# Decode attention on one core: the last group's output products as three column tiles, and the second last slab folded on GpSimd

## The chip, the core and the metric

The kernel runs on one NeuronCore of a Trainium2 chip. A core has five instruction streams: PE (TensorE, matrix products), DVE (VectorE), ACT (ScalarE), POOL (GpSimd) and SP (SyncE, which here only issues transfers), and 16 DMA engines that bring data from HBM into the core's SBUF. Products land in PSUM, a memory of banks of 512 fp32 columns on 128 partitions. The metric is the device time of one execution in microseconds (us), the median of several runs.

## What is computed

Two independent problems, A and B, of the same shape. Each takes one new token for two batch entries and attends to the last 4096 positions of a key and value cache:

```python
B, Sq, D = 2, 1, 576
Hq, Hkv, Sk, Dh = 32, 16, 16384, 128
W = min(4096, max(256, Sk // 4))            # 4096
q = (x @ wq).reshape(B, Sq, Hq, Dh)         # bf16 throughout
k = k_cache[:, :, Sk - W:, :]               # each kv head serves two q heads
v = v_cache[:, :, Sk - W:, :]
scores = einsum(q, k) * Dh ** -0.5
p = softmax(scores)
o = einsum(p, v)                            # (2, 1, 32 * 128)
result = o @ wo                             # (2, 1, 576)
```

The results of A and B stand side by side in an output of 2 x 1 x 1152 in bf16.

## The kernel before

**Slabs.** A problem's 2 x 16 kv heads are read in eight slabs each for K and V; a slab is four (batch, head) pairs of 4096 positions, 4 MB, laid out as 128 partitions (4 pairs x 32 rows) by 128 positions of 128 numbers. With two problems there are 16 slabs (ND = 16, numbered 0 to 15), and two slabs form a group (NG = 8): group G has slabs 2G and 2G+1 and covers four q heads of each half of the heads, for both batch entries. K and V slabs go through a ring of four SBUF buffers, and SP issues the load of the next slab when the buffer's last reader is done. The order of the loads is the list `stream`; the last V slab (15) comes in two pieces, positions 0 to 95 and 96 to 127 (`PIECES`).

**One slab.** DVE transposes K in four parts (L494), PE makes the scores in PSUM tile `st` (L519, and L171 where the weights stay loaded), DVE takes the maximum (L529), ACT the exponential with its row sums (L564), DVE transposes the probabilities (L572), and PE multiplies them with V into `acc` (L610): 32 matmuls of 512 columns, four at a time on column tiles of 32 partitions in the one bank.

**Folding.** `acc` holds the sum over positions in 4 x 32 rows, of which only the matching blocks count. ACT copies it to `acc_sb` (L622). For every slab but the last two, GpSimd masks the copy with `maskJ` (L629) and adds its four blocks in two steps (L632, L637) into `acc_r`, and PE adds over partitions with `maskS` (`comb`, L650). For slabs 14 and 15, PE does both with four matmuls against columns of `ident_r` (L657). DVE multiplies with the reciprocal sums (`norm`, L674 and L692).

**Output projection.** For every group but the last, the normalised heads are spread by a mask (`spread`, L683), gathered by PE (`redist`, L708) and copied by ACT into `Rsb` (L716), which regroups eight rows of heads so that the group's 1024 rows of wo can be read as long packets (`wob`). PE then multiplies `Rsb` with `wob` (L743 for 512 columns into `ot`, L171 for the other 64 into a small bank `tb`), summed over groups in PSUM and in `o_rest`. The last group (7) is split: slab 14 goes through spread (L696) and `redist` and covers four of the eight rows, slab 15 comes directly from `norm` as `oTn` (four heads). Its products (L747) are two halves of 288 columns: `fin(0)` on PSUM partitions 0 and 1 of the first bank of slab 14's score tile `st`, `fin(1)` on partitions 32 and 33 of its second bank. Before them, the sums of groups 4 to 6 are copied there from `ot` and `tb` by ACT (L767) and DVE (L768, L770), so that the products add to them. Then ACT and DVE copy one half each to `out_sb` (L779, L780), and ACT and SP issue a transfer for each half (L788).

**The last weights.** Behind the two pieces of V 15, SP issues the last group's wo rows: 512 rows for slab 14 (L284), then for the four heads of slab 15 three loads (`HEADS`: heads 0 and 1, head 2, head 3; L268). Head 2's load is split by rows into five transfers (`ROWS`: 8, 4, 2, 2 and 112 rows).

**Order.** Every operation is added to one engine's list with its dependencies, and the lists run in the order of the calls; a wait holds all that stands behind it on its engine. Small PE results alternate between two banks `tb` (`tb_job`), and a job waits until the bank's last result was read. After the loop over slabs, the order is written out by hand:

```python
do_PV(ND - 2, range(NRD), None)
do_comb(D_)                    # slab 13
do_norm(D_)
do_comb(ND - 2)
do_redist(D_ // 2)             # group 6
do_norm(ND - 2)
do_proj(D_)                    # group 6
...
do_PV(D_, ..., pieces[0])      # slab 15
do_redist(D_ // 2)             # group 7, slab 14
do_PV(D_, ..., pieces[1])
do_comb(D_); do_norm(D_)
do_proj(ND - 2); do_proj(D_)
```

Of the kernel before, what the change touches and what calls it, by code (L numbers as in the profile page):

```python
# [59 lines left out]
def build_kernel(nc, probs, out, cfg=None):  # L60
# [30 lines left out]
    NOUT = wo0.shape[1]  # L91
    NH = NOUT // 2
    NB0 = 512
    NB1 = NOUT - NB0
    assert NOUT % 2 == 0 and 0 < NB1 <= NB0
    SCALE = float(Dh) ** -0.5
# [3 lines left out]
    HEADS = [(0, 1), (2,), (3,)]  # L100
    ROWS = [(0, 8), (8, 12), (12, 14), (14, 16), (16, 128)]
    NPC = len(PIECES)

    def by_group(G):
        return G < NG - 1

    es = ExitStack()
    with es:
# [40 lines left out]
        ident_r = sb("ident_r", [128, 32], BF16)  # L149
        out_sb = sb("out_sb", [Bb, NPROB, NOUT], BF16)  # L150
        ps = lambda name, shape: es.enter_context(nc.psum_tensor(name, shape, FP32))
# [12 lines left out]
        wl_sem = [sem("wl%d" % n_) for n_ in range(len(HEADS))]  # L164
        part_sem = [sem("part%d" % n_) for n_ in range(len(ROWS) - 1)]
        out_sem = sem("outdone")
# [18 lines left out]
        def load_x(P, eng):  # L185
# [3 lines left out]

        p_ones_b = S.add("pool", lambda e: e.memset(ones_b[:], 1.0), [], "ones_b")  # L190
        p_ident_b = S.add("pool", lambda e: e.affine_select(ident_b[:], ones_b[:], [[-1, 128]], ALU.is_equal, 0.0,
# [3 lines left out]
        p_ones_f = S.add("dve", lambda e: e.memset(ones_f[:], 1.0), [], "ones_f")  # L195
        p_ident_f = S.add("pool", lambda e: e.affine_select(ident_f[:], ones_f[:], [[-1, 128]], ALU.is_equal, 0.0,
                                                           base=0, channel_multiplier=1), [p_ones_f], "ident_f")
        x_zd = S.add("dve", lambda e: e.memset(x_dup[:].rearrange("b h r t -> b (h r t)"), 0.0), [], "zero_xdup")
# [60 lines left out]
        def issue_last(woP, pc, r0, deps):  # L259
            for n_, hs in enumerate(HEADS):  # L260
                ops = []
                for i, (d0, d1) in enumerate(ROWS if n_ == 1 else [(0, 128)]):
                    sem_h = wl_sem[n_] if d1 == 128 else part_sem[i]

                    def f(e, hs=hs, d0=d0, d1=d1, sem_h=sem_h):
                        t, r = divmod(hs[0], 2)
                        row = t * HH + r0 + 256 + 128 * r
                        return e.dma_start(wob[d0:d1, pc, 4 + hs[0]:4 + hs[0] + len(hs), :],  # L268
                                           woP[row:row + 128 * len(hs), :].rearrange("(h d) n -> d h n", d=128)[d0:d1]).then_inc(sem_h, 16)
                    ops.append(dma_op("sp", sem_h, 1, f, deps, "wl%d_%d" % (n_, i)))  # L270
                wo_last.append(ops)

# [302 lines left out]
        def do_rsel(G):  # L575
            d = [chain[(2 * G, "exp")], chain[(2 * G + 1, "exp")], init["maskS"]]
            if G >= 1:
                d.append(chain[(G - 1, "tot")])
            chain[(G, "rsel")] = S.add("pool", lambda e: e.tensor_tensor(  # L579
                rsel[:, :, :], maskS[:].unsqueeze(1).broadcast_to([128, 2, 8]),  # L580
                rsum[:].unsqueeze(2).broadcast_to([128, 2, 8]), ALU.mult), d, "rsel%d" % G)
# [15 lines left out]
        def do_PV(D_, rounds, wait):  # L597
# [20 lines left out]
            if rounds[-1] == last_r:  # L618
                d = [op]
                if D_ >= 2:  # L620
                    d.append(acc_r_ev[D_ - 2])
                acc_ev[D_] = S.add("act", lambda e: e.activation(acc_sb[:, D_ % 2, :], ACC[:, :], ACTF.Copy), d, "accev%d" % D_)  # L622
                G = D_ // 2
                if not by_group(G) or (D_ % 2 == 0 and G < NG - 2):
                    return
                l0, l1 = (0, 2) if G < NG - 2 else (D_ % 2, D_ % 2 + 1)
                a_ = acc_sb[:, l0:l1, :]
                v = a_.rearrange("k l (j d) -> k l j d", j=4)
                t = S.add("pool", lambda e: e.tensor_tensor(  # L629
                    v, v, maskJ[:].unsqueeze(1).unsqueeze(3).broadcast_to([128, l1 - l0, 4, 128]), ALU.mult),  # L630
                    [acc_ev[2 * G + l] for l in range(l0, l1)] + [init["maskJ"]], "accm%d" % D_)
                t = S.add("pool", lambda e: e.tensor_tensor(a_[:, :, 0:256], a_[:, :, 0:256], a_[:, :, 256:512], ALU.add),  # L632
                          [t], "acca%d" % D_)
                d = [t]
                if G >= 1:
                    d.append(comb[2 * G - 1])
                t = S.add("pool", lambda e: e.tensor_tensor(  # L637
                    acc_r[:, l0:l1, :], a_[:, :, 0:128], a_[:, :, 128:256], ALU.add), d, "accr%d" % D_)
                for l in range(l0, l1):
                    acc_r_ev[2 * G + l] = t  # L640

        def do_comb(D_):
            if by_group(D_ // 2):
                if D_ % 2 == 0:
                    return

                def fg(e, bank):
                    last = None
                    for l_ in range(2):
                        last = e.matmul(bank[:, 8 * l_:8 * l_ + 8], acc_r[:, l_, :], maskS[:, :], start=True, stop=True)  # L650
                    return last
                n, bank, comb[D_] = tb_job(fg, "comb%d" % D_, [acc_r_ev[D_ - 1], acc_r_ev[D_], init["maskS"]])
            else:
                def fl(e, bank):
                    last = None
                    for j4 in range(4):
                        last = e.matmul(bank[:, 0:8], acc_sb[:, D_ % 2, 128 * j4:128 * j4 + 128], ident_r[:, 8 * j4:8 * j4 + 8],  # L657
                                        start=(j4 == 0), stop=(j4 == 3))
                    return last
                n, bank, comb[D_] = tb_job(fl, "comb%d" % D_, [acc_ev[D_], init["ident_r"]])  # L660
            comb_at[D_] = (n, bank)
# [59 lines left out]

        def fin(half):
            return ST[(ND - 2) % 2][32 * half:32 * half + Bb, 512 * half:512 * half + NH]

        def do_proj(D_):
# [8 lines left out]
            else:  # L734
                parts = [([(oTn[:, h, :], 4 + h) for h in hs], [norm[D_]] + wo_last[n_], False, False, n_ == len(HEADS) - 1)
                         for n_, hs in enumerate(HEADS)]
            for lhs, deps, start, rstart, rstop in parts:
                def f(e, rest, lhs=lhs, start=start, rstart=rstart, rstop=rstop):
                    last = None
                    for n_, (l_, s_) in enumerate(lhs):  # L740
# [4 lines left out]
                        else:  # L745
                            for half in range(2):
                                last = e.matmul(fin(half), l_, wob[:, pc, s_, half * NH:(half + 1) * NH],  # L747
                                                start=False, stop=end, skip_group_check=True)
                    return last
                deps = deps + [e_ops[(P - 1, 0)]]  # L750
                if by_group(G):
                    n, bank, proj[D_] = tb_job(f, "proj%d" % D_, deps)
                    rest_at[G] = bank
# [11 lines left out]
                    elif G == NG - 2:  # L765
                        d = [proj[D_], chain[(ND - 2, "exp")], chain[(ND - 2, "max")]]
                        a_ = S.add("act", lambda e: e.activation(fin(0), OT[0:Bb, 0:NH], ACTF.Copy), d, "fin0")  # L767
                        tb_consumer[n] = S.add("dve", lambda e: e.tensor_tensor(  # L768
                            fin(1)[:, NB0 - NH:NH], o_rest[:, :], bank[0:Bb, 0:NB1], ALU.add), d + [rest_add[G - 1]], "fin1")
                        fin_ops.append(S.add("dve", lambda e: e.tensor_copy(fin(1)[:, 0:NB0 - NH], OT[0:Bb, NH:NB0]), [a_], "fin2"))  # L770
                    else:
# [4 lines left out]
        def do_E(P):  # L776
            G = (P + 1) * GPP - 1
            if G == NG - 1:
                e_ops[(P, 0)] = S.add("act", lambda e: e.activation(out_sb[:, P, 0:NH], fin(0), ACTF.Copy), [proj[2 * G + 1]], "Elo%d" % P)  # L779
                e_ops[(P, 1)] = S.add("dve", lambda e: e.tensor_copy(out_sb[:, P, NH:NOUT], fin(1)), [proj[2 * G + 1]], "Ehi%d" % P)  # L780
                return
# [76 lines left out]
        do_comb(D_)  # L858
        do_norm(D_)
        do_comb(ND - 2)  # L860
        do_redist(D_ // 2)
        do_norm(ND - 2)
        do_proj(D_)
        D_ = ND - 1
        issue_until(len(stream) - 1)
        do_PV(D_, range(PIECES[0][0] // JR, PIECES[0][1] // JR), pieces[0])
        do_redist(D_ // 2)
        do_PV(D_, range(PIECES[1][0] // JR, PIECES[1][1] // JR), pieces[1])
# [5 lines left out]
        for P in range(NPROB - 1):  # L874
            do_out(P, 0, NOUT, "sp", [e_ops[(P, 0)], e_ops[(P, 1)]])
        do_out(NPROB - 1, 0, NH, "act", [e_ops[(NPROB - 1, 0)]])
        do_out(NPROB - 1, NH, NOUT, "sp", [e_ops[(NPROB - 1, 1)]])

# [99 lines left out]
```

## Time and profile before

| | |
|---|---|
| time, median of 3 runs | 363.62 us (363.61 to 363.75) |
| the profiled execution's own time | 363.54 us |
| its span, first to last instruction | 362.3 us |
| PE, DVE, ACT, POOL busy | 63%, 56%, 19%, 10% |
| HBM read | 153.10 MB, 423 GB/s over the span |
| mean granted TensorE clock | 0.854 |
| first product of the last group | 358.46 us |
| copies to `out_sb` | 360.52 us |

Times in the profile are counted from the first instruction. A row of a timeline has start, length, engine, line of the kernel, operation and tiles (out<-in), and in square brackets how long the engine was idle before and what ended that. A group of several instructions has xN; its length is then that of the whole group. In a table of stages, each engine has its busy time and in brackets its number of instructions, and the last three columns are the granted clock, the DMA engines' share and their traffic.

### The profile page before, as it was taken

The numbers are of one execution on the slowest core, as the hardware profiler recorded it, in microseconds if no ns is written. First come the engines' busy times: TensorE is split into PE (matmuls) and PEld (weight loads), VectorE is DVE, ScalarE is ACT, GpSimd is POOL, SyncE is SP. The second block draws the span as 40 slices with busy tenths as digits, with TensorE's granted clock in tenths as the row PEclk, the third lists the DMA queues.
The fourth block names the chain that finished last, engine by engine and source line by source line (L and its number), as shares of the span: only waits on it lengthen the run. The fifth ranks groups of instructions, "written<-read, shape, count | busy, mean of one in ns | idle before, by whom it ended". The sixth has DMA issues, their size and how long they took to land.

```text
span 362.3 us, 2770 instructions
## 1 busy us (share of the span) xinstructions
PE 228.3 (63%) x1324; PEld 58.8 (16%) x954; DVE 201.7 (56%) x176; ACT 68.8 (19%) x153; POOL 35.4 (10%) x55
## 2 busy tenths in 40 slices
PE   0398195576866647374874737685672748666774
PEld 0010021112221212111220201111120112211121
DVE  3113598473918476391926557192945739189830
ACT  1046402020300302020200203112120203002131
POOL 1000000003000040004000040001200040100020
PEclk9999589787796969889688968869897897969997
DMA  8999999999999999999999999999999999999995
GB/s 348 416 452 409 459 401 447 438 409 453 422 431 434 420 445 425 438 427 423 431 435 434 431 422 434 434 434 429 411 447 434 434 429 423 431 438 427 436 408 224
DMA packets 7087, 153.27 MB, mean 423 GB/s; under 512 B 794, under 2 KB 1316, under 8 KB 1700
## 3 DMA queue, kind: packets, MB, share of 16 engines
q1 hardware_dynamic: 7068, 153.10, 98.7%
q8 instruction: 9, 0.15, 0.2%
q14 instruction: 2, 0.02, 0.0%
q10 hardware_dynamic: 8, 0.00, 0.0%
HBM read 153.10 MB, written 0.00 MB: 423 GB/s over the span
## 4 chain that ended last, share of the span: by engine, by line
DMA 71%; DVE 14%; PE 14%; SPq 1%; issue 0%; ACT 0%; DVEq 0%
DMA ring<-in_B_k_cache_dram 34%; DMA ring<-in_A_k_cache_dram 26%; DVE xt L494 13%; DMA wob<-in_B_wo_dram 8%; PE st L171 5%; PE st L519 4%; DMA x_sb<-in_B_x_dram 3%; PE st L430 1%; PE ot L171 1%; PE acc L171 1%; PE tb L171 1%; PE tb L430 1%; PE st L747 1%; DVE nM L542 1%; PE tb L532 0%
## 5 line engine op out<-in xcount | busy, mean ns | idle before, releaser
L494 DVE STREAM_TRANSPOSE xt<-ring 128x2048 f32<-128x2048 f32 x64 | 145.4, 2285 | 75.9 <-DMA ring<-in_B_k_cache_dram 39.0
L519 PE MATMUL st<-xt,zq 128*128 128x512 bf16 x256 | 116.8, 456 | 111.4 <-DVE xt L494 85.1
L171 PE MATMUL st<-xt,zq 128*128 128x512 bf16 x256 | 115.4, 451 | 0.0
L519 PEld LDWEIGHTS st<-xt,zq 128*128 128x128 bf16 x256 | 28.1, 110 | 207.5 <-DVE xt L494 99.5
L610 PE MATMUL acc<-ring,pC 128*32 128x512 bf16 x512 | 34.9, 390 | 2.6 <-DMA ring<-in_B_v_cache_dram 2.5
L547 ACT ACTIVATE nMrep<-nM 1x128 f32<-1x128 f32 x16 | 4.9, 308 | 140.1 <-DVE nM L542 140.1
L622 ACT ACTIVATE acc_sb<-acc 128x512 bf16<-128x512 f32 x16 | 9.5, 596 | 80.9 <-PE acc L610 80.9
L572 DVE STREAM_TRANSPOSE pC<-pR 128x1024 bf16<-128x1024 bf16 x16 | 19.5, 1219 | 4.0 <-ACT pR L564 2.1
L529 DVE TENSOR_REDUCE m<-st 128x1 f32<-128x1024 f32 x16 | 19.0, 1190 | 1.4 <-PE st L171 1.4
L629 POOL TENSOR_TENSOR acc_sb<-acc_sb,maskJ 128x1024 bf16<-128x1024 bf16 (+1 forms) x8 | 13.4, 1681 | 60.6 <-ACT acc_sb L622 60.6
L481 POOL TENSOR_TENSOR zq<-qk,maskA 128x128 bf16<-128x128 bf16 x16 | 6.4, 401 | 125.9 <-PE st L171 104.5
L564 ACT ACTIVATE pR<-st,bias_sb 128x1024 bf16<-128x1024 f32 x16 | 17.8, 1114 | 0.5
L454 DVE STREAM_TRANSPOSE qtr<-qrow 128x512 f32<-128x512 f32 x8 | 5.7, 711 | 21.0 <-ACT qrow L444 13.7
L395 ACT ACTIVATE st<-maskB 128x1024 f32<-128x1024 bf16 x16 | 16.5, 1032 | 1.6 <-POOL rsel L579 0.4
L743 PE MATMUL ot<-wob,Rsb 128*2 128x512 bf16 x56 | 15.9, 402 | 0.3 <-DVE om L696 0.3
L610 PEld LDWEIGHTS acc<-ring,pC 128*32 128x32 bf16 x512 | 13.1, 97 | 16.4 <-DMA ring<-in_B_v_cache_dram 3.2
L579 POOL TENSOR_TENSOR rsel<-maskS,rsum 128x16 f32<-128x16 bf16 x8 | 1.7, 218 | 124.0 <-ACT pR L564 124.0
L171 PE MATMUL tb<-wob,Rsb 128*2 128x64 bf16 x56 | 11.1, 199 | 0.0
L362 PE MATMUL tb<-ident_b,x_sb 4*128 4x4 bf16 x4 | 0.3, 174 | 14.2 <-DVE x_dup L369 14.2
L632 POOL TENSOR_TENSOR acc_sb<-acc_sb 128x512 bf16<-128x512 bf16 (+1 forms) x8 | 8.2, 1031 | 0.6
L762 DVE TENSOR_TENSOR o_rest<-o_rest,tb 2x64 f32<-2x64 f32 x3 | 0.6, 209 | 13.8 <-PE tb L171 13.8
L542 DVE TENSOR_REDUCE nM<-tb 1x8 f32<-1x128 f32 x16 | 4.4, 273 | 6.4 <-PE tb L532 6.4
(83 smaller groups left out, 109.6 us busy)
## 6 DMA issues: line engine op xcount, KB each, us to landing
ring<-in_A_k_cache_dram SPq DMA_DIRECT2D x8, 4096.0 KB, 30.7
ring<-in_A_v_cache_dram SPq DMA_DIRECT2D x8, 4096.0 KB, 32.6
ring<-in_B_k_cache_dram SPq DMA_DIRECT2D x8, 4096.0 KB, 30.7
ring<-in_B_v_cache_dram SPq DMA_DIRECT2D x7, 4096.0 KB, 32.4
wob<-in_A_wo_dram SPq DMA_DIRECT2D x4, 1152.0 KB, 33.8
ring<-in_A_wq_dram SPq DMA_DIRECT2D x1, 4096.0 KB, 12.8
ring<-in_B_wq_dram SPq DMA_DIRECT2D x1, 4096.0 KB, 22.5
wob<-in_B_wo_dram SPq DMA_DIRECT2D x3, 1152.0 KB, 33.5
```

What stands on the lines that cost most here:

```text
L171: return e.add_instruction(mybir.InstMatmult(name=nc.get_next_instruction_name(), engine=i.engine, ins=[e.lower_ap(rhs), i.ins[1]], outs=[ ...
L395: chain[(s, "fill")] = S.add("act", lambda e: e.activation(ST[s % 2][:, :].rearrange("k (h j) -> k h j", h=2), maskB[:].unsqueeze(1).broad ...
L494: Xop[(s, u)] = S.add("dve", lambda e: e.transpose(xt[:, i % NKT, :].rearrange("k (j w) -> k j w", w=64), ring[:, n % NR, :].bitcast(FP32) ...
L519: first = last = e.matmul(bank, zq[:, p4, s % NZQ, w0:w0 + 128], mv, start=False, stop=stop, skip_group_check=True)
L529: chain[(s, "max")] = S.add("dve", lambda e: e.tensor_reduce(m1[:, 0:1], ST[s % 2][:, :], AX.X, ALU.max), d, "max%d" % s)
L564: chain[(s, "exp")] = S.add("act", lambda e: e.activation(pR[:, :], ST[s % 2][:, :], ACTF.Exp, bias=bias_sb[:, 0:1], scale=SCALE, accum_ou ...
L572: chain[(s, "pC")] = S.add("dve", lambda e: e.transpose(pC[:, s % NPT, :, :].rearrange("k j c -> k (j c)"), pR[:, :]), d, "pC%d" % s)
L610: last = e.matmul(ACC[32 * cb:32 * cb + 32, 0:512], pC[:, D_ % NPT, j0_:j0_ + 4, :].rearrange("k j c -> k (j c)"), ring[:, n % NR, j0_ * 1 ...
L622: acc_ev[D_] = S.add("act", lambda e: e.activation(acc_sb[:, D_ % 2, :], ACC[:, :], ACTF.Copy), d, "accev%d" % D_)
L629: t = S.add("pool", lambda e: e.tensor_tensor(v, v, maskJ[:].unsqueeze(1).unsqueeze(3).broadcast_to([128, l1 - l0, 4, 128]), ALU.mult), [a ...
L632: t = S.add("pool", lambda e: e.tensor_tensor(a_[:, :, 0:256], a_[:, :, 0:256], a_[:, :, 256:512], ALU.add), [t], "acca%d" % D_)
L743: first = e.matmul(OT[0:Bb, 0:NB0], l_, wob[:, pc, s_, 0:NB0], start=start and begin, stop=end, skip_group_check=True)
```

## The change

- The last group's products run as three tiles of 192 columns (`NT`, `NTC`) on PSUM partitions 0, 32 and 64 of one bank, in place of two of 288 in two banks. The sums of the earlier groups are copied there by three ACT copies and one DVE addition, which now waits for the last of the copies; the DVE copy that followed goes.
- One DVE copy takes all three tiles, partitions 0 to 65, to a new buffer `out_t`. Two transfers, one on SP and one on ACT, each bring one batch entry out, three pieces of 192 numbers.
- Slab 14 is folded on GpSimd by the same three instructions as slabs 12 and 13, and its `comb` becomes one matmul. In the order by hand, the group 6 steps come first, then `comb`, `norm` and `redist` of slab 14, all of it ahead of slab 15's PV products. Some small PE jobs stay on the bank that the job before them used.
- Head 2's weights come as one transfer; `ROWS` and its semaphores go.
- At the start, `ones_b` is filled by DVE and `ident_f` is a DVE copy of `ident_b`; both were GpSimd's. `rsel` of groups 0 and 7 goes from GpSimd to DVE.

```diff
+    NT = 3
+    NTC = NOUT // NT
...
-    ROWS = [(0, 8), (8, 12), (12, 14), (14, 16), (16, 128)]
...
-        p_ones_b = S.add("pool", lambda e: e.memset(ones_b[:], 1.0), [], "ones_b")
+        p_ones_b = S.add("dve", lambda e: e.memset(ones_b[:], 1.0), [], "ones_b")
...
+        p_ident_f = S.add("dve", lambda e: e.tensor_copy(ident_f[:], ident_b[:]), [p_ident_b], "ident_f")
...
-            chain[(G, "rsel")] = S.add("pool", lambda e: e.tensor_tensor(
+            chain[(G, "rsel")] = S.add("pool" if 0 < G < NG - 1 else "dve", lambda e: e.tensor_tensor(
...
+            elif D_ < ND - 1:
+                n, bank, comb[D_] = tb_job(lambda e, bank: e.matmul(bank[:, 0:8], acc_r[:, 0, :], maskS[:, :], start=True, stop=True),
+                                           "comb%d" % D_, [acc_r_ev[D_], init["maskS"]])
...
-        def fin(half):
-            return ST[(ND - 2) % 2][32 * half:32 * half + Bb, 512 * half:512 * half + NH]
+        def fin(t):
+            return ST[(ND - 2) % 2][32 * t:32 * t + Bb, 0:NTC]
...
-                            for half in range(2):
-                                last = e.matmul(fin(half), l_, wob[:, pc, s_, half * NH:(half + 1) * NH],
+                            for t in range(NT):
+                                last = e.matmul(fin(t), l_, wob[:, pc, s_, t * NTC:(t + 1) * NTC],
                                                 start=False, stop=end, skip_group_check=True)
...
-                        a_ = S.add("act", lambda e: e.activation(fin(0), OT[0:Bb, 0:NH], ACTF.Copy), d, "fin0")
+                        for t in range(NT):
+                            c0, c1 = t * NTC, min((t + 1) * NTC, NB0)
+                            a_ = S.add("act", lambda e, t=t, c0=c0, c1=c1: e.activation(fin(t)[:, 0:c1 - c0], OT[0:Bb, c0:c1], ACTF.Copy), d, "fin%d" % t)
                         tb_consumer[n] = S.add("dve", lambda e: e.tensor_tensor(
-                            fin(1)[:, NB0 - NH:NH], o_rest[:, :], bank[0:Bb, 0:NB1], ALU.add), d + [rest_add[G - 1]], "fin1")
-                        fin_ops.append(S.add("dve", lambda e: e.tensor_copy(fin(1)[:, 0:NB0 - NH], OT[0:Bb, NH:NB0]), [a_], "fin2"))
+                            fin(NT - 1)[:, NTC - NB1:NTC], o_rest[:, :], bank[0:Bb, 0:NB1], ALU.add), [a_, rest_add[G - 1]], "finr")
+                        fin_ops.append(tb_consumer[n])
...
-                e_ops[(P, 0)] = S.add("act", lambda e: e.activation(out_sb[:, P, 0:NH], fin(0), ACTF.Copy), [proj[2 * G + 1]], "Elo%d" % P)
-                e_ops[(P, 1)] = S.add("dve", lambda e: e.tensor_copy(out_sb[:, P, NH:NOUT], fin(1)), [proj[2 * G + 1]], "Ehi%d" % P)
+                e_ops[(P, 0)] = S.add("dve", lambda e: e.tensor_copy(
+                    out_t[0:32 * (NT - 1) + Bb, :], ST[(ND - 2) % 2][0:32 * (NT - 1) + Bb, 0:NTC]), [proj[2 * G + 1]], "Eout%d" % P)
...
+        do_fold(ND - 2)
+        do_redist(D_ // 2)
+        do_proj(D_)
         do_comb(ND - 2)
-        do_redist(D_ // 2)
         do_norm(ND - 2)
-        do_proj(D_)
+        do_redist(ND // 2 - 1)
...
-        do_redist(D_ // 2)
...
-        do_out(NPROB - 1, 0, NH, "act", [e_ops[(NPROB - 1, 0)]])
-        do_out(NPROB - 1, NH, NOUT, "sp", [e_ops[(NPROB - 1, 1)]])
+        for b in range(Bb):
+            P = NPROB - 1
+            dma_op("act" if b else "sp", out_sem, 1, lambda e, b=b: e.dma_start(
+                out[b, 0, P * NOUT:(P + 1) * NOUT].rearrange("(t c) -> t c", t=NT), out_t[b:32 * (NT - 1) + b + 1:32, :]).then_inc(out_sem, 16),
+                [e_ops[(P, 0)]], "out%d_b%d" % (P, b))
```

`do_fold` holds the three GpSimd instructions that stood at the end of `do_PV` (L629 to L640), unchanged but for being callable for slab 14.

## Prediction

> **What bounds the kernel now.** I read the page first, for the engine and DMA shares, then the chain of waits over the last 40 us, then the timeline of the last 15 us, then a table of busy times by stage.
>
> The page's DMA rows say that the kernel is one long read: every slice between the first and the last is at 9 tenths, and the traffic is 153 MB at 423 GB/s.
>
> ```profile
> span 362.3 us, 2770 instructions
> ...
> PEclk9999589787796969889688968869897897969997
> DMA  8999999999999999999999999999999999999995
> ```
>
> No engine is near full (PE 63%, DVE 56%, GpSimd 10%), so an edit before the last slab lands is worth nothing unless it delays the issue of a transfer; K slabs land 30.7 us after their issue, which is how much delay the queue swallows. Only what follows the reads can be saved. The chain of waits shows that tail (start, length, what):
>
> ```profile
> 330.00 28.42 DMA wob<-in_B_wo_dram
> 358.42 0.04 issue
> 358.46 2.04 PE st L747 x16
> 360.49 0.02 issue
> 360.52 0.45 DVE out_sb L780
> ```
>
> After 358.42 there are 2.04 us of wo products, 0.45 us of copy, and then 1.3 us for the output's flight to the span's end at 362.27. The timeline shows the products in two batches, and the last transfer's issue:
>
> ```profile
> 332.97 0.43 SPq L268 DMA_DIRECT2D wob<-in_B_wo_dram  x1
> 358.46 1.06 PE L747 MATMUL st<-wob,Rsb 128*2 128x288 bf16 x8
> 359.34 1.13 PE L747 MATMUL st<-wob,oTn 128*2 128x288 bf16 x8
> 360.52 0.40 ACT L779 ACTIVATE out_sb<-st 2x288 bf16<-2x288 f32 x1 [2.46 <-PE st L747]
> 360.52 0.45 DVE L780 CAST out_sb<-st 2x288 bf16<-2x288 f32 x1 [1.95 <-PE st L747]
> ```
>
> In the second batch pairs start every 0.24 us (359.55, 359.79, 360.03): the two halves run side by side, and 288 columns in 240 ns is 1.2 columns per ns. The clock is the reason; the stage table shows it granted at 1.00 up to 358.56 and 0.50 after (the column behind the x counts):
>
> ```profile
> 355.15:358.56 3.41, 1.74 (x28) 0.60 (x22) 0.16 (x1) 0.78 (x2) 0.00 (x0) 1.00 0.91 332
> 358.56:361.98 3.42, 1.92 (x16) 0.63 (x12) 0.46 (x2) 0.40 (x1) 0.00 (x0) 0.50 0.13 44
> ```
>
> One more clock matters, the landing of the last weights (head 3): issue 332.97 plus 26.8 from the page of DMA issues is 359.75 us. The last pair starts at 360.03, so it is PE-bound by 0.28 us only. That caps what faster products can give.
>
> **The change, part by part.**
>
> *Three tiles instead of two.* Removed: 8 pairs of 288 columns; added: 8 trios of 192, with 24 weight loads for 16. At half clock a trio should take 192/1.2 = 160 ns if three tiles stream side by side as two do. That four can, in one bank, is seen in the PV products: 32 matmuls of 512 columns on 32-column tiles take 1.91 us at full clock, 215 ns for each four, with four loads inside. So the first four heads run from 358.46 to about 359.07. Heads 0 and 1 wait for their weights: issue 330.64 plus 28.6 is 359.2; they start at 359.25 and 359.41, head 2 at 359.57. Head 3 is ready at 359.73, but its weights are not: from here the transfer, not PE, sets the start.
>
> *The removed row split.* Head 2's weights come as one transfer of 128 rows, where 16 rows went ahead in four small ones. Most late queues then carry 8 of its rows where they carried 7. A row's packet of 1152 B takes 51 ns in the trace, one every 47 ns, so head 3 lands at 359.80 instead of 359.75. Both ends: 0 (if the split's own overhead balances it) and 0.09 (one packet where packets were slowest, at 86 ns). I take 0.05. Four SP issues of about 0.3 us go; they lie 26 us ahead of their landing, worth nothing.
>
> *The last trio and its end.* It starts 0.04 us after the landing (the first pair did: 358.42 to 358.46), at 359.84. A 288-column matmul lasts 0.444 us at half clock; 96 columns less at 0.833 ns is 0.364. With 0.01 for the third tile it ends at 360.21, against 360.47 before: 0.26 us gained. If trios kept the pairs' 240 ns, head 3 would start at 360.03 as now, and only the shorter last matmul, 0.07, would be left.
>
> *One copy.* Before, ACT and DVE each copied 288 columns, DVE being later (0.45). Now DVE alone reads 66 partitions by 192 columns. DVE's PSUM copies here: 2x64 0.212, 2x224 0.391, 2x288 0.449; between the first two a column costs 1.12 ns, so 192 cost 0.355. Partitions do not count: the 128x1024 reduction takes 1.19, or 1.04 ns a column plus what every instruction carries. Gain 0.09, with ends of 0.08 and 0.12. The Trainium skill (TensorEngine Tiling, "PSUM Bottleneck") advises to share the emptying of PSUM between ScalarE and VectorE after tiling, and the change does the reverse. The same section also advises vectorizing over tiles; if instead the 576 columns cost in sequence, the copy would be an estimated 0.78 us, and the sum would be a loss of 0.07.
>
> *The output.* Two issues stay, one on ACT and one on SP, now both behind the DVE copy; each moves three pieces of 384 B, not two of 576 B. Of the two before, SP's came last, issued at 360.99 and ending the span 1.27 us later. ACT's, issued 0.05 earlier, no longer has a head start but is no later than SP's. A third piece of about 28 ns per issue bounds the cost above at 0.06, a parallel start below at -0.05; I take -0.02.
>
> *The fold of slab 14 on GpSimd.* Four small matmuls go from PE; three GpSimd instructions come: 1.04, 0.67 and 0.43 us by the rows of the neighbouring slab. They can start when ACT has emptied the slab at 349.56 and end at 351.75. PE needs them only after the products of slab pair 6, which end at 352.66, so 0.9 us covers them.
>
> *The moved redistribution.* It now stands ahead of slab 15's PV products on PE, so it can hold them. It waits for a chain: three ACT copies after 352.70 instead of one (0.30 + 0.30 + 0.26, from 2x288 0.362 and 128x16 0.174), then DVE's addition, which now waits for them (0.22), and behind it in DVE's queue the norm (0.16) and the spread (0.42), then PE (0.2): 354.75 with handovers. The first PV piece, which started at 354.30 on its landing, then runs 354.75 to 356.25. The second lands at 356.75, so the cover is 0.5 us; if it were gone, the end would move only after another 0.3 us, since the first four heads finish 0.2 us ahead of the next weights and PE has 0.1 to spare at head 3.
>
> *The rest.* ones_b to DVE and ident_f as a DVE copy lie before 5 us, and DVE then idles 9.7 us for x. rsel on DVE for pairs 0 and 7 adds some 0.2 us ahead of a transpose; its PV products wait for a landing 6 us later. Nothing.
>
> **Sum.** Products 0.26, copy 0.09, rest 0: 0.35; with 0.02 for the output (about half of what its parallel start may save) 0.37. The span goes from 362.27 to 361.90. The profiled execution took 363.54, 1.27 beyond its span, and the median of the runs is 0.08 above it: 363.62 - 0.37 = 363.25 us.
>
> **Rivals.**
>
> *The clock stays full.* The window that preceded the drop had 1.74 us of PE work, the one before it 1.77 and no drop; the change shifts about 0.45 us of PV into the later one. Then the last trio lasts 0.193 + 128 x 0.417 = 0.246 us (from 64 columns 193 ns and 512 columns 380 ns at full clock) in place of 0.364: 363.13. Against it: other windows with 1.4 to 1.9 us went either way. Chance 0.25.
>
> *Small output pieces cost a second trip.* In the trace the pieces leave at 361.7 to 361.8 and the span ends at 362.27, so a write and its answer take some 0.45 us. Were a piece of 384 B read, merged and written, I would add that once: 363.70. No row here shows such a write. The Trainium skill (DMA: Bandwidth & Descriptors, "Specifications") gives 512 B as the least size at line rate, with read-modify-write below, so it speaks against the change. By that rule the gain would be lost. Chance 0.08.
>
> *The tiles take turns in one bank.* Before, the two halves wrote two banks; now three tiles write one. If they took turns, a head would need 3 x 160 = 480 ns at half clock; from 358.46 the eight would end at 362.5, 2.0 us later than 360.47; less 0.09 for the copy that is 365.55, clearly slower. It decides from 0.25 us a head: 358.46 + 7 x 0.25 + 0.37 is 360.58, the old end plus the copy's gain. Against it: the four PV tiles in one bank. Chance 0.04.
>
> *The weights land later.* If the reads end 0.3 us later than worked out (uneven queues without the split, slower packets), the PE part of the gain is gone and the copy stays: about 363.55. Chance 0.08.
>
> **How the numbers follow.** The forecast as summed has 0.45. The last 0.10 is for the stream of reads itself, which I can't work out: it ends up to 1 us earlier or later because another build meets the queues otherwise. A difference of 0.2% is 0.73 us, about what a measurement of this kernel can tell from no change; the forecast is half of that. Faster by over 0.2% needs the full clock, a shorter copy and an earlier landing together, or a better stream: 0.24. Slower by over 0.2% needs the turns, the chain ahead of PV running over, or a worse stream: 0.14. Within: 0.62. The range goes from the full clock with 0.3 us of better landing, 362.80, to the second trip with small losses, 363.80.
>
> **What would show it.** Right: L747's successor has 24 matmuls with trios 160 ns apart in the first batch; the last trio begins 0.04 us after the last wob landing near 359.8; one DVE copy of 66x192 near 0.35 us; both output issues start together; the redistribution near 354.6 and PV's second piece still ended by its landing. Wrong: the last trio directly behind the one before (PE still the bound), a granted clock of 1.00 to the end, PV held beyond 356.8, or a flight of over 1.3 us after the copy.

## The result, and the profile after

The change made the kernel slower: 366.56 us (median of 6 runs, 364.93 to 367.5) against 363.69 for the kernel before, measured with it, a ratio of 1.0075 [1.0053, 1.0098]. Forecast was 363.25, within 362.8 to 363.8.

The profiled execution took 366.49 us with a span of 364.5, so 1.99 lie outside the span, where it was 1.27. The page, with the rows shown of before (the last DMA slice falls from 5 tenths to 3: the reads are over earlier in a longer span):

```profile
span 364.5 us, 2773 instructions
...
PE 225.8 (62%) x1328; PEld 58.4 (16%) x959; DVE 202.1 (55%) x179; ACT 69.0 (19%) x154; POOL 36.5 (10%) x54
...
PEclk9999699897886989889696969889688968869986
DMA  8999999999999999999999999999999999999993
```

The tail of the chain of waits (start, length, what) no longer begins with a landing. From 350.27 until the output is issued it is one row of compute steps:

```profile
350.27 1.17 DVE om L685
...
354.98 0.28 ACT st L771
...
356.18 0.44 DVE om L698
...
356.67 0.22 PE tb L710 x2
356.88 3.37 PE acc L605 x24
...
360.28 0.61 ACT acc_sb L617
...
360.93 0.26 PE tb L659 x4
361.18 0.78 PE st L749 x24
...
361.99 0.35 DVE out_t L783
```

Line 685 is the spread product of group 6 (L683 before), 698 the spread of slab 14, 710 the redistribution, 605 slab 15's PV products, 749 the wo products. The last weights land at 359.69 by the page of DMA issues (359.74 before); the products, which they should have set, start at 361.11, since PV is done at 360.22 only. The timeline of the same execution has the two ends of the story:

```profile
350.11 1.04 POOL L628 TENSOR_TENSOR acc_sb<-acc_sb,maskJ 128x512 bf16<-128x512 bf16 x1 [0.41 <-ACT acc_sb L617]
350.27 1.16 DVE L685 TENSOR_TENSOR om<-oTg,maskD 128x256 bf16<-128x256 bf16 x1
...
361.44 0.50 PE L749 MATMUL st<-wob,oTn 128*2 128x192 bf16 x12
361.99 0.35 DVE L783 CAST out_t<-st 66x192 bf16<-66x192 f32 x1 [0.60 <-PE st L749]
362.37 0.82 SPq L883 DMA_DIRECT2D out_dram<-out_t  x1
362.38 0.81 ACTq L883 DMA_DIRECT2D out_dram<-out_t  x1
```

DVE's product took 0.43 us before (349.58). Here GpSimd's mask product of slab 14, which the change added, had started 0.16 us earlier, and DVE's takes 1.16: it ends 0.28 after GpSimd's. At the other end, each output issue takes 0.82 us instead of 0.25. In the table of stages (PE, PE loads, DVE, ACT, GpSimd; then granted clock, DMA share, GB/s) the clock falls in between:

```profile
349.65:353.06 3.41, 1.50 (x13) 0.65 (x9) 1.40 (x3) 0.56 (x2) 2.24 (x4) 1.00 1.00 428
353.06:356.48 3.42, 2.00 (x11) 0.48 (x4) 0.59 (x3) 0.79 (x3) 0.00 (x0) 0.50 0.92 376
356.48:359.89 3.41, 3.23 (x34) 1.25 (x34) 0.13 (x1) 0.18 (x1) 0.00 (x0) 0.50 0.61 222
359.89:363.30 3.41, 1.34 (x36) 0.69 (x28) 0.52 (x2) 0.60 (x1) 0.00 (x0) 1.00 0.00 0
```

The difference of the two executions, 2.95 us, adds up as follows: the products end 1.46 later (361.94 for 360.48), the copy is 0.10 shorter, from the copy's end to the span's end it is 0.84 longer (2.16 for 1.31), 0.72 lies outside the span, and 0.03 is handover.

### The profile page after: what moved, and what is told of

It is laid out like the page before. It is cut to its first block, busy times and chain, and to the rows that moved or that the text cites. A ratio compares the mean times of both kernels' runs of the same rounds, so it can differ in the third digit from the quotient of the medians.

```text
span 364.5 us, 2773 instructions
## 1 busy us (share of the span) xinstructions
PE 225.8 (62%) x1328; PEld 58.4 (16%) x959; DVE 202.1 (55%) x179; ACT 69.0 (19%) x154; POOL 36.5 (10%) x54
## 4 chain that ended last, share of the span: by engine, by line
DMA 63%; DVE 17%; PE 16%; ACT 2%; issue 1%; POOL 1%; SPq 0%; DVEq 0%; ACTq 0%
DMA ring<-in_B_k_cache_dram 34%; DMA ring<-in_A_k_cache_dram 26%; DVE xt L489 14%; PE st L172 6%; PE st L514 4%; DMA x_sb<-in_B_x_dram 3%; PE st L425 1%; PE acc L605 1%; PE ot L745 1%; PE tb L172 1%; ACT pR L559 1%; DVE m L524 1%; PE ot L172 1%; PE tb L425 1%; PE acc L172 1%
## 5 line engine op out<-in xcount | busy, mean ns | idle before, releaser
L628 POOL TENSOR_TENSOR acc_sb<-acc_sb,maskJ 128x1024 bf16<-128x1024 bf16 (+1 forms) x9 | 14.5, 1608 | 94.0 <-ACT acc_sb L617 94.0
L745 PE MATMUL ot<-wob,Rsb 128*2 128x512 bf16 x56 | 16.8, 419 | 0.3 <-ACT Rsb L718 0.3
L631 POOL TENSOR_TENSOR acc_sb<-acc_sb 128x512 bf16<-128x512 bf16 (+1 forms) x9 | 9.0, 995 | 0.7
```

Of the source, the lines that this page charges most:

```text
L628: t = S.add("pool", lambda e: e.tensor_tensor(v, v, maskJ[:].unsqueeze(1).unsqueeze(3).broadcast_to([128, l1 - l0, 4, 128]), ALU.mult), [a ...
L745: first = e.matmul(OT[0:Bb, 0:NB0], l_, wob[:, pc, s_, 0:NB0], start=start and begin, stop=end, skip_group_check=True)
```

## The experiments

Three costs had to be separated: the chain ahead of PV, the output's issue, and the time outside the span. Each row compares with the kernel before on the same chip (its medians: 363.56 to 363.87 us; span 362.2 to 362.4; outside 1.3). "Outside" is a run's time less its span.

| label | what | median us [range] | ratio [95%] | span | outside |
|---|---|---|---|---|---|
| after | the change | 366.56 [364.93, 367.5] | 1.0075 [1.0053, 1.0098] | 364.6 | 1.97 |
| e1_redist_back | after, redistribution back between the PV pieces | 364.63 [364.36, 365.30] | 1.0016 [1.0003, 1.0030] | 362.6 | 2.00 |
| e9_fold_waits | after, GpSimd's product waits for DVE's | 364.63 [363.96, 364.89] | 1.0018 [1.0001, 1.0035] | 362.6 | 1.99 |
| e2_fold_pe | after, slab 14 folded on PE | 365.53 [364.11, 365.90] | 1.0034 [1.0017, 1.0051] | 363.9 | 1.61 |
| e3_out_by_tile | after, output tile by tile | 364.04 [363.57, 366.08] | 1.0013 [0.9993, 1.0033] | 362.0 | 1.98 |
| e4_two_tiles | after, two tiles | 366.23 [364.22, 366.76] | 1.0044 [1.0022, 1.0066] | 364.5 | 1.95 |
| e7_tiles_batch_out | before + tiles, output by batch entry | 364.05 [363.88, 365.54] | 1.0008 [0.9994, 1.0023] | 362.8 | 1.28 |
| e8_tiles_tile_out | before + tiles, output tile by tile | 363.57 [363.34, 366.00] | 0.9998 [0.9976, 1.0020] | 362.25 | 1.29 |
| e11_piece_pairs | before + tiles, output in unlike pairs | 364.02 [363.95, 364.30] | 1.0002 [0.9990, 1.0015] | 362.75 | 1.31 |
| e6_start_alone | before + moves at the start | 363.86 [363.56, 365.63] | 1.0009 [0.9991, 1.0027] | 362.25 | 1.62 |
| e10_four_memsets | before + four idle DVE fills | 364.18 [363.57, 365.61] | 1.0012 [0.9997, 1.0027] | 362.25 | 2.01 |
| e5_fold_alone | before + fold and order | 363.61 [363.24, 365.38] | 1.0005 [0.9987, 1.0024] | 362.3 | 1.25 |
| e12_start_and_fold | e6 + e5 | 364.24 [363.57, 365.98] | 1.0019 [1.0000, 1.0038] | 362.3 | 1.93 |
| e13_three_mended | after, all three costs removed | 363.40 [363.17, 363.58] | 0.9989 [0.9975, 1.0003] | 362.1 | 1.29 |

### The chain ahead of PV: e1, e2, e9

e1 leaves the whole chain as it is, but PV no longer stands behind it:

```diff
-        do_redist(ND // 2 - 1)          # after do_norm(ND - 2)
...
         do_PV(D_, range(PIECES[0][0] // JR, PIECES[0][1] // JR), pieces[0])
+        do_redist(D_ // 2)
```

> The changed kernel with one step put back: slab 14's redistribution stands between the two PV pieces again, as before the change; fold, tiles and output stay changed. Theory 1 (the redistribution, queued ahead of PV behind a chain that ends at 356.7, holds the PV products until they run at half clock, 356.8 to 360.2): the PV products start at their landing near 354.4 and end near 357.5, the wo products end about 1.3 to 1.6 us earlier, time near 365.1. Rival 2 (the loss is the output alone): time stays at 366.5. Rival 3 (the clock, not the queue): PV starts early but the time falls by less than 0.5.

The median span fell from 364.6 to 362.6 (ten runs). In the timeline PV starts on its landing again, at full clock, the products end at 360.05, and the output's issue is as long as ever:

```profile
354.31 1.48 PE L605 MATMUL acc<-ring,pC 128*32 128x512 bf16 x24 [1.64 <-DMA ring<-in_B_v_cache_dram]
...
359.04 1.01 PE L749 MATMUL st<-wob,oTn 128*2 128x192 bf16 x12
360.48 0.82 SPq L883 DMA_DIRECT2D out_dram<-out_t  x1
```

The profile alone doesn't show that the new place did it. In this execution slab 13 ended early and DVE's product was first, as it was before the change:

```profile
349.48 0.43 DVE L685 TENSOR_TENSOR om<-oTg,maskD 128x256 bf16<-128x256 bf16 x1
349.64 1.16 POOL L628 TENSOR_TENSOR acc_sb<-acc_sb,maskJ 128x512 bf16<-128x512 bf16 x1 [0.74 <-ACT acc_sb L617]
```

Slab 14's spread ended at 354.23, so PV would hardly have been held in the order of the change either. e2 and e9 keep the redistribution ahead of PV. e2 takes slab 14 off GpSimd:

```diff
-        do_fold(ND - 2)
...
-            elif D_ < ND - 1:           # do_comb: one matmul on acc_r
```

> The changed kernel with slab 14 folded on PE by four matmuls again (no GpSimd work after slab 13's), the order by hand as changed. Theory 2 (the fold on GpSimd slows DVE's mask product of group 6, L685, from 0.43 to 1.16 us, because both use the same way into SBUF): L685 back at 0.43, the redistribution 0.7 us earlier or more, time down by 0.7 to 1.5, near 365.3. Rival (the fold is covered): L685 still over 1 us, or the time unchanged at 366.5.

Slab 13 ended late here, as in the change: the product of line 685 (682 here) started at 350.18. It took 0.42 us again, the redistribution came at 354.98 and PV ran from 355.12 at full clock. The time hardly followed, though. In the profiled execution the lateness came from elsewhere: one of 16 transfer queues landed its part of the weights 1.4 us after the others, and the products waited for it.

```profile
361.10 0.64 PE L746 MATMUL st<-wob,oTn 128*2 128x192 bf16 x6 [1.23 <-DMA wob<-in_B_wo_dram]
```

The profiles of e8 and e10 show the same wait (1.46 and 1.41 us). Of 108 executions of the kernel before, 24 have spans of 363.3 or more, longer by about as much, but none of them was profiled. In e2 eight of ten spans were long, and one of them was profiled. So e2 clears the chain in its profile and leaves its own time open. e9 asks the same without moving work: GpSimd's product of slab 14 waits for DVE's.

```diff
-                [acc_ev[2 * G + l] for l in range(l0, l1)] + [init["maskJ"]], "accm%d" % D_)
+                [acc_ev[2 * G + l] for l in range(l0, l1)] + [init["maskJ"]]
+                + ([spread[G - 1]] if D_ == ND - 2 else []), "accm%d" % D_)
```

> The changed kernel with one wait more: GpSimd's mask product of slab 14 waits until DVE's mask product of group 6 (L685) is done, so that DVE always goes first. The redistribution stays ahead of PV. Theory 2 (the chain is late because GpSimd, where it starts first, makes DVE take 1.16 us, and the idle PE then loses its clock): L685 at 0.43 in every clock phase, the redistribution near 354.5 to 355.3, PV at full clock, time as with the redistribution put back, 364.6. Rival (the queue position alone): the chain still ends after 356 and the time stays near 366.5.

```profile
349.45 0.42 DVE L685 TENSOR_TENSOR om<-oTg,maskD 128x256 bf16<-128x256 bf16 x1
350.03 1.04 POOL L628 TENSOR_TENSOR acc_sb<-acc_sb,maskJ 128x512 bf16<-128x512 bf16 x1 [1.15 <-DVE om L685]
...
354.39 1.48 PE L605 MATMUL acc<-ring,pC 128*32 128x512 bf16 x24
```

All eight spans lie at 362.9 or below, their median 2.0 us under the change, with the redistribution still ahead of PV (354.25) and the fold still on GpSimd. The profile is no test of the wait, though: slab 13 ended early, and slab 14's copy was done at 349.58 only, so DVE would have been first without it. The test with a late slab 13 is e13, below. Against e9, the change's redistribution is 2.42 us later (356.67): 0.82 because slab 13 ended later in that execution, 0.73 in the product itself, and 0.85 because the clock fell at 353.06 while the products of group 6 were running (from their start to ACT's copy 3.01 us, not 2.16). Then PV, at half clock, took 3.41 us.

### The output: e3, e4, e7, e8, e11

e3 sends the same three tiles as three transfers, each of two pieces from neighbouring partitions:

```diff
-        for b in range(Bb):
-            P = NPROB - 1
-            dma_op("act" if b else "sp", ..., out_t[b:32 * (NT - 1) + b + 1:32, :] ...)
+        for t in range(NT):
+            dma_op("act" if t == 1 else "sp", ..., out_t[32 * t:32 * t + Bb, :] ...)
```

> The changed kernel with the last output as three transfers of 2 pieces of 384 B (one for each tile; SP, ACT, SP) in place of two of 3 pieces. Theory 3a (three pieces make the issue long: 0.82 us, not 0.25): issues near 0.25 each, span after the copy near 1.5 us in place of 2.1, time down by 0.5. Theory 3b (pieces of 384 B are what costs): issue and flight stay long, time unchanged or 0.2 up. Theory 3c (code loading near the end): issues long in whichever instruction comes first, and the time beyond the span stays at 2.0.

Each issue took 0.25 to 0.26 us, not 0.82. The median span, 362.0, fell further than this explains: in the profiled execution DVE's product was first (349.44, 0.43 us), so the chain was not late either. Up to its output e3 is the change itself, and eight of its ten spans lie at 362.7 or below. So which product comes first is not fixed by the order of the work, and the short spans of e1 and e9 are weaker evidence than they look. e4 goes the other way, with two pieces of 576 B per transfer, 32 partitions apart:

```diff
-    NT = 3
+    NT = 2
```

> The changed kernel with two tiles of 288 columns in one bank in place of three of 192: two ACT copies ahead, 16 matmuls, one DVE copy of 34x288, two transfers of 2 pieces of 576 B. Theory 3a and 3b: issues 0.25, flight after the copy 1.3; the copy 0.45; time down by about 0.7. If the time beyond the span is tied to the output it falls from 2.0 to 1.25 as well, and the time by 1.4. Theory 3c: no change in issue or beyond the span. Theory 1 adds 0.3 us at most, as the ACT copies are two.

```profile
362.41 0.45 DVE L783 CAST out_t<-st 34x288 bf16<-34x288 f32 x1 [0.91 <-PE st L749]
362.88 0.62 SPq L883 DMA_DIRECT2D out_dram<-out_t  x1
```

0.62 us for two pieces of the size that took 0.25 before: neither their number alone nor their size is the reason. The chain was lost here as in the change (DVE's product 1.15, PV 3.60 us from 356.73), which repeats it without the three tiles. e7 and e8 put the tiles on the kernel before, with the two forms of output (edit abridged):

```diff
+    NT = 3; NTC = NOUT // NT            # fin(t), three matmuls, one copy to out_t
+        for b in range(Bb): ...         # e7: as the change
+        for t in range(NT): ...         # e8: as e3
```

> The kernel before with the three tiles, the one copy and the output by batch entry as changed (pieces from partitions 32 apart); order, fold, weights and start as before. Theory 3 (an issue costs 0.2 us for each piece that comes from a partition 32 away, as 2 pieces cost 0.60 and 3 cost 0.82): issues of 0.82, 2.1 us from the copy's end to the span's end, the wo products 0.3 us shorter, span near 362.6. Time 363.9 if 1.3 lies beyond the span, 364.6 if the output makes it 2.0. Rival (the output cost came from the late chain): issues of 0.25, span near 361.9, time 363.2.

> As the run with tiles and output by batch entry, but the output goes in three transfers, one for each tile, two pieces from neighbouring partitions each. Theory 3: issues of 0.26, 1.55 us from the copy's end to the span's end, span near 361.9, time 363.2, 0.4 below before and the best of all. Rival 3b (pieces under 512 B cost): a longer flight, 2.1 us, no better than the other output.

e7's timeline has the products' end at 360.3, the copy to 360.66 and the issue of 0.82 again, and its span ends 2.16 us after the copy:

```profile
360.69 0.82 SPq L883 DMA_DIRECT2D out_dram<-out_t  x1
```

By the medians, e7's span is 0.55 longer than e8's. e8's profile is of an execution with a late queue (products held 1.46 us by a landing), but its output can be read: issues of 0.25, 0.26 and 0.25, the span's end 1.5 us after the copy and 1.2 after the last issue. e11 tells number from neighbourhood: on e7, SP first sends partitions 0 and 33 together and ACT 64 and 65, then each one single partition (edit in words).

```diff
+   sp:  out_t[0:34:33, :]        act: out_t[64:66, :]
+   sp:  out_t[1:2, :]            act: out_t[32:33, :]
```

> The kernel before with three tiles and one copy, and the output in four transfers: SP first takes the pieces of partitions 0 and 33 (which lie apart in the output too), ACT partitions 64 and 65, then SP partition 1 alone and ACT partition 32 alone. Theory 3s (the long issue comes from source partitions that are not neighbours): SP's first issue 0.60, ACT's first 0.26, the single ones below 0.26. Theory 3d (it comes from pieces that join up in the output): SP's first 0.26 too.

```profile
360.69 0.72 SPq L885 DMA_DIRECT2D out_dram<-out_t  x1
360.69 0.25 ACTq L885 DMA_DIRECT2D out_dram<-out_t  x1
```

Two pieces from partitions 0 and 33 cost 0.72, two from 64 and 65 cost 0.25, single ones 0.27 (ACT) and 0.41 (SP). A transfer from SBUF rows that aren't neighbours is what takes long to issue here; why the two single ones differ stays open.

### Outside the span: e6, e10

e6 takes the moves alone: `ones_b`, `ident_f` and two `rsel` on DVE (edit abridged).

```diff
-        p_ones_b = S.add("pool", ...memset(ones_b[:], 1.0)...)
+        p_ones_b = S.add("dve", ...memset(ones_b[:], 1.0)...)
-        p_ident_f = S.add("pool", ...affine_select(ident_f...)...)
+        p_ident_f = S.add("dve", ...tensor_copy(ident_f[:], ident_b[:])...)
+            rsel: "pool" if 0 < G < NG - 1 else "dve"
```

> The kernel before with only the moves off GpSimd: ones_b and ident_f at the start and rsel of groups 0 and 7 on DVE. Theory 1 and 3 give nothing: span 362.3, 1.3 beyond it, time as before within 0.2. Rival 4 (the moves lengthen what lies outside the span, by another split of instructions over the engines): span 362.3, 2.0 beyond it, time 0.7 up.

The span stayed at 362.25 and the time outside it rose from 1.3 to 1.62: half of the change's excess. Its page has 180 DVE instructions for 176. e10 adds only four DVE fills of a buffer that nobody reads:

```diff
+        for i in range(4):
+            S.add("dve", lambda e, i=i: e.memset(pad[:, 2*i:2*i+2], 0.0), [], "pad%d" % i)
```

> The kernel before with four DVE memsets of 128x2 more, at the start, where DVE is idle; nothing uses them. Theory 4a (time beyond the span grows with DVE's number of instructions, 180 to 184, as in the run with the start alone): 1.65 beyond the span, time 0.35 up. Theory 4b (it is what the moved instructions are, or GpSimd's fewer ones): 1.3 beyond the span, time as before.

```profile
PE 225.6 (62%) x1323; PEld 58.0 (16%) x954; DVE 201.6 (55%) x180; ACT 68.7 (19%) x153; POOL 35.3 (10%) x55
```

2.01 us outside, the whole of the excess. Over all kernels the time outside is 1.3 where DVE has 176 instructions or fewer (e5, e7, e8, e11, e13), 1.6 where it has 179 or 180 and GpSimd 51 (e2, e6), and 2.0 where DVE has as many and GpSimd 54 or 55 (the change, e1, e3, e4, e9, e10, e12). That four more DVE instructions are enough is shown by e10, whose own two forecasts (1.65 or 1.3) both missed. Whether it is their number or their place is not shown, since e6, e10 and the change all add some at the start. Neither is what they cause, nor whether GpSimd's count matters or only goes along with it.

### The fold without the rest: e5, e12

In words:

```diff
 e5:  before + do_fold, do_comb and the order by hand of the change
 e12: e5 + the moves of e6
```

> The kernel before with one part of the change alone: slab 14 folded on GpSimd and the order by hand as changed (redistribution ahead of PV); tiles, output, weights and start as before. Theory 1 with 2 (GpSimd's mask product and DVE's mask product of group 6 race; where GpSimd starts first DVE needs 1.16 us, the chain ends late, and PV follows at half clock): two kinds of runs, spans near 362.3 and near 364, and a profile that shows which came first on the side of its span. Rival (the chain is late through the three ACT copies): all runs near 362.3, time as before. Beyond the span: 1.3 if it hangs on output or start, 1.7 to 2.0 if on GpSimd's three instructions.

> The kernel before with the start moves and slab 14's fold with its order, no tiles, no new output, weights in five. Beyond the span: 2.0 if start and fold together make it (theory 4c, as 1.65 with the start alone, 1.3 with the fold alone), 1.65 if the rest of the change (output, single transfer of weights) brings the last 0.35. Spans near 362.2, and near 363.7 where PV meets the half clock or a transfer queue is late.

e5 is where the theory of the race had to give way in part. GpSimd's product was first, DVE's took 1.20, and PV started at 356.49, as late as in the change. Nothing was lost:

```profile
349.69 1.04 POOL L633 TENSOR_TENSOR acc_sb<-acc_sb,maskJ 128x512 bf16<-128x512 bf16 x1 [0.45 <-ACT acc_sb L622]
349.81 1.20 DVE L690 TENSOR_TENSOR om<-oTg,maskD 128x256 bf16<-128x256 bf16 x1
...
356.49 1.91 PE L610 MATMUL acc<-ring,pC 128*32 128x512 bf16 x32
```

PV took 1.91 us at full clock and was done at 358.40, ahead of the last weights; the span is 362.2. e12 shows the same (product 1.16, PV 356.26 to 358.17, span median 362.3). The clock differs from the change: in e5 it was half from 352.21 to 355.62 only, during the products of group 6, and in e12 it stayed at 1.00 from 326.7 until after the last product. So in these two profiles a late PV at full clock cost nothing, and in the change and e4 it met the half clock and cost the time. All profiles fit a loss that needs both, but no run moved the clock alone. Three of e5's ten spans and two of e12's lie near 364; none of them was profiled, so what lengthened them is open.

### All three mended: e13

The change with e9's wait, e3's output, and the moves of e6 undone (edit abridged):

```diff
+                + ([spread[G - 1]] if D_ == ND - 2 else []), "accm%d" % D_)
+        for t in range(NT): ...         # output as e3
-        p_ones_b, p_ident_f, rsel on DVE
+        p_ones_b, p_ident_f, rsel on GpSimd
```

> The changed kernel with the three costs found taken out at once: GpSimd's mask product of slab 14 waits for DVE's of group 6, the output goes tile by tile in three transfers, and ones_b, ident_f and rsel are GpSimd's again; the fold on GpSimd, the order, the tiles, the one copy and the single transfer of weights stay. If the three are all of it: span 361.9, 1.3 beyond it, most runs near 363.2 to 363.3, level with before or 0.1 to 0.3 below it. If something else is left in the change: over 363.9.

```profile
350.50 0.42 DVE L686 TENSOR_TENSOR om<-oTg,maskD 128x256 bf16<-128x256 bf16 x1
351.07 1.04 POOL L629 TENSOR_TENSOR acc_sb<-acc_sb,maskJ 128x512 bf16<-128x512 bf16 x1 [1.15 <-DVE om L686]
...
355.43 2.08 PE L606 MATMUL acc<-ring,pC 128*32 128x512 bf16 x32
...
359.83 0.25 PE L750 MATMUL st<-wob,oTn 128*2 128x192 bf16 x3 [0.16 <-DMA wob<-in_B_wo_dram]
360.12 0.35 DVE L784 CAST out_t<-st 66x192 bf16<-66x192 f32 x1 [1.45 <-PE st L750]
360.50 0.56 SPq L884 DMA_DIRECT2D out_dram<-out_t  x2
```

363.40 us, 3.2 below the change, and all twelve spans at 362.3 or below: with the three costs away nothing of the loss is left. Slab 13 ended late here too (DVE's product at 350.50), and slab 14's copy was done at 350.31. In the change GpSimd started 0.08 after that copy, so without the wait it would have been first again by about 0.1. With the wait there was no collision, the redistribution came at 355.30 and PV ran at full clock. This profile and e2's are the ones that show the collision at work: late slab 13, no collision, no loss in the chain. Against the kernel before the ratio is 0.9989 [0.9975, 1.0003]: 0.16 us less, which can't be told from no change. The last trio does start on the landing of the weights and lasts 0.25, as one rival had it, and the copy ends 0.50 earlier than in the profile of before (360.47), but 0.22 of that is given back between it and the span's end (1.53 for 1.31), where SP now has two issues in a row (0.56).

## Why the prediction was wrong

- **Failed: "0.9 us covers them" for the fold, and the chain ahead of PV.** The three GpSimd instructions did have their cover; what I didn't ask was which DVE instruction would run beside the first of them. The trace of before had the answer: I took 349.56 as GpSimd's start, and DVE's spread product started at 349.58. In the change DVE's product came 0.7 later. Slab 14's PV, which had waited for its landing before (347.00), started at 347.48, only 0.5 later, so that GpSimd led by 0.16. A product of 0.43 became 1.16. The Trainium skill (GPSIMD Engine Reference, "Specifications") says that GpSimd shares its SBUF interfaces with VectorE and contends with DVE instructions that have two SBUF inputs; line 685 has two (`oTg`, `maskD`), and the trace agrees: 1.15 to 1.20 in the four profiles where GpSimd was first (the change, e4, e5, e12), 0.42 or 0.43 where DVE was. I hadn't weighed that rule.
- **Failed: "three ACT copies after 352.70", and with it the cover of "0.5 us" and "another 0.3 us".** The steps of that chain were sized well: 1.69 us from the first copy to the redistribution, where my terms with their handovers give 1.85. Its start was wrong: I kept it from before, and it moved to 354.98. Of these 2.28 us, 0.69 are slab 13's later end, 0.73 the product and 0.85 the group 6 products at half clock. The redistribution came at 356.67 instead of 354.6.
- **Failed: where the half clock falls.** I treated the clock as a matter of the last products only. It was the group 6 products and PV that met it: PV took 3.41 us instead of 1.91 and ran past the landing of the weights. The last products, which I had at half clock, ran at 1.00 from 359.89, which I had given as a sign of being wrong and a rival with a chance of 0.25. In e5 PV ended at 358.40, 1.0 later than before and 0.7 past my cover, and nothing was lost; but its last products ran at full clock too, so that is no measure of the cover as I had summed it.
- **Failed: the output, "-0.02".** It cost 0.84 in the profile and about 0.55 between the medians of e7 and e8. I priced the third piece by its bytes; the cost is in the issue, which rows of before could not show, since both issues there read neighbouring partitions.
- **Failed: "Nothing" for the moves at the start.** They cost nothing inside the span. "1.27 beyond its span" was taken as fixed, and it isn't: 1.6 with them alone, 2.0 with the rest.
- **Right: the tiles do not take turns.** Trios start 82 ns apart at full clock (four in 0.33 us, from 361.11 to 361.44), so that rival is out. The whole 24 matmuls take 0.83 us, where 16 took 2.04 with waiting. The rival of the full clock had 0.246 for the last matmul: it measured 0.246.
- **Right: the copy.** 0.353 for 0.355. **Not decided: the row split's +0.05.** The last weights landed at 359.69, 0.05 earlier than before, and at 359.67 to 359.68 in e1, e3 and e9. In e13 the last trio, which waited for them, started at 359.83, so they landed about 0.1 later there. The term is smaller than this spread.
- **Out: the second trip of small pieces.** From e8's last issue to its end it takes 1.2 us with pieces of 384 B, 1.27 before with 576. By the Trainium skill's 512 B rule (DMA: Bandwidth & Descriptors, "Specifications"), as I read it for that rival, it would have been longer; no run here shows that.
- **The range** missed because it held the unknowns of terms I had, and none for a second engine on the same memory. Of the forecast gain of 0.37, e13, where the three costs are away, shows 0.16, which its interval doesn't tell from none; the gain as such stays unproven.

Why the race tips the clock is argued, not shown: in the change the stage from 349.65 to 353.06 held only 1.50 us of PE work, and the clock was half in the next. The Trainium skill (TensorE: Matmul & The Clock Gate, "What's actually happening") has windows of 3.4 us that run free of the kernel's start; the traces agree: the clock falls at 353.06 and is back at 359.89 here, twice 3.41 us later, it falls at 352.21 and is back at 355.62 in e5, once 3.41, and before the change it falls at 358.56. So two executions of one build can fall on either side, which may be why the change's six spans reach from 362.9 to 365.6. What makes slab 13 end late is open. It is no fixed cost of the change: e1, e3 and e9 are the change up to that point and had DVE's product at 349.44 to 349.48, while e2, e4, e12 and e13 had it at 350.18 to 350.91.

## What to carry to other kernels

Before work is given to an idle engine, list what the neighbouring engine does in the same microsecond, by start times and not by busy shares: two products that could start 0.02 us apart by the trace are a race, and a wait that fixes their order (e9, e13) left the chain on time. A transfer's price includes its issue: let each transfer read neighbouring partitions, even if that needs one transfer more. And compare time less span between kernels before a difference is looked for in the trace.

## What was unexpected of the hardware

- A DVE product with two SBUF inputs, 0.43 us by itself, takes 1.15 to 1.20 when GpSimd's product of 1.04 us has started 0.12 to 0.17 us before it; when DVE is first, it keeps its 0.42 or 0.43, and GpSimd's takes 1.16 (e1, started 0.16 after DVE's) or 1.04 (e3, 0.28 after).
- Issuing a small output transfer took 0.25 us for two pieces from neighbouring partitions, 0.60 to 0.72 for two from partitions 32 or 33 apart, and 0.82 for three.
- Four idle DVE fills of two numbers per partition each lengthened the run by 0.7 us outside the span (e10). Why stays open.
- In the profiles of e2, e8 and e10 the last products wait 1.2 to 1.5 us for weights of one late transfer queue. 24 of 108 executions of the kernel before have spans longer by about as much. The cause stays open.
